# A GELU feed-forward block with its gradients on one core: four-tile transposing loads past the rows' ends, and another order of the opening loads

## The chip, the cores and the metric

The kernel runs on one core of one Trainium2 chip. The metric is the device time of one execution in microseconds; the median of three runs before the change is 280.55 us (280.51 to 280.58).

## The reference

```python
def _fwd_reference(x, w1, b1, w2, b2):
    h = jnp.einsum("bsd,df->bsf", x, w1) + b1
    h = _gelu(h)                       # tanh form
    return jnp.einsum("bsf,fd->bsd", h, w2) + b2

def reference(x, w1, b1, w2, b2, grad_out):
    _out, _vjp = jax.vjp(_f, x, w1, b1, w2, b2)
    _grads = _vjp(grad_out)
    return (_out, *_grads)
```

All arrays are bf16: x and grad_out (g below) 1 x 2048 x 448, w1 448 x 1792, w2 1792 x 448, b1 1792, b2 448. Six outputs are wanted: the forward result, and the gradients of x, w1, b1, w2 and b2.

## The kernel before

**Sizes.** The 2048 rows are cut into four blocks of 512 (SB). F = 1792 is 14 tiles of 128, taken as 7 pairs. D = 448 is three full tiles and a tail of 64 (KF = 3, DL = 64). One step is one pair of one block, so there are 28 steps.

**A step.** With u = x w1 + b1 and q = g w2^T (both held transposed, F on the partitions), step i issues on PE: the full tiles of u for step i + 2 (L159), the tails of that u and of q of step i (L169, L174; contractions over 64 rows, which sit in different halves of the array), the full tiles of q (L184), and then some matmuls of finished pairs for output rows (`ps_o`) and x-gradient rows (`ps_x`), both L255. ACT copies u out of PSUM with the bias (L193) and makes gelu(u) into `hT` (L199), a square (L203) and a tanh (L211). DVE makes the derivative of gelu from these (L207 to L220), and L224 multiplies it with q out of PSUM into `ghT`. Two PSUM buffers of the pool `psq` are used in turn, in effect one for u and one for q: q of step i + 1 can start only when L224 of step i has read q of step i, and u of a step when the copies of the one before are done. The order is written out by hand (a manual schedule), and each engine works through its own instructions in that order.

**Loads.** x and g are needed with D on the partitions, w2 too. Each of these is brought by transposing DMAs on SP's queue: one for the three full tiles, and one for the tail, whose 128 columns overlap the full tiles by 64 (L90 and L91 for x, L97 and L98 for g, L109 and L110 for w2). In `xT` the tail of x lies in partitions 64 to 127; in `gT` and `w2T_t` the tail lies in partitions 0 to 63. w1 (L102, with its 64 tail rows by L103) and w2 as it is (`w2_sb`, L106) come by plain loads. All of them are issued in program order on SP's queue, apart from w1's first two parts, which ACT's queue issues. `w1T_sb` (w1 transposed, L138) is first needed by the x gradient. Eight semaphores are used in turn for the loads of SP and ACT: a load is issued only when the eighth before it has landed.

**Opening.** Ten matmuls on zeros (L143) warm PE up. Then u of steps 0, 1 and 2, output matmuls of pair 0, q of step 0, output matmuls of pair 1, and the loop over steps 1 to 27. In the first block every step takes the next pair of w1, of w2 transposed and of w2, so each part of the weights has a step at which it is first wanted.

**Later.** `turn_gh` (L236) turns finished pairs of `ghT` by transposing DMAs into `gh_nat`; gelu results are stored to DRAM by POOL's queue (L231) and read back transposed (L382). The next blocks of x and g are loaded in steps 8, 10, 14 and 16. After step 27 come the rest of the output and x-gradient rows, then the gradient of w1 (L430, L441) and that of w2 (L454).

Of the kernel before, what the change touches and what calls it, by code (L numbers as in the profile page):

```python
# [19 lines left out]
def kernel(  # L20
# [15 lines left out]
    nc = tc.nc  # L36
# [12 lines left out]
    NSTEP = NB * NPAIR  # L49
    LEAD = 2  # L50
    SYNC_DEP = mybir.DependencyInfo(mybir.DependencyClass.Sync, mybir.DependencyReason.DATA)

# [22 lines left out]
    w1_f = const.tile([P, KF, F], BF16, name="w1_f")  # L75
    w2T_f = const.tile([P, KF, F], BF16, name="w2T_f")
    wt1 = const.tile([P, F], BF16, name="wt1")
    w2T_t = const.tile([P, F], BF16, name="w2T_t")
    w2_sb = const.tile([P, NF, D], BF16, name="w2_sb")
# [5 lines left out]
    xT, gT = {}, {}  # L85

    def load_x(b):
        t = blk.tile([P, KF + 1, SB], BF16, name="xT", tag="xT")
        rows = slice(b * SB, (b + 1) * SB)
        nc.sync.dma_start_transpose(out=t[:, 0:KF, :], in_=x2[rows, 0:KF * P])  # L90
        nc.sync.dma_start_transpose(out=t[:, KF, :], in_=x2[rows, D - P:D])  # L91
        xT[b] = t

    def load_g(b):
        t = blk.tile([P, KF + 1, SB], BF16, name="gT", tag="gT")
        rows = slice(b * SB, (b + 1) * SB)
        nc.sync.dma_start_transpose(out=t[:, 0:KF, :], in_=g2[rows, DL:D])  # L97
        nc.sync.dma_start_transpose(out=t[:, KF, :], in_=g2[rows, 0:P])  # L98
        gT[b] = t

    def load_w1(eng, f0, f1):
        eng.dma_start(out=w1_f[:, :, f0:f1], in_=w1[0:KF * P, f0:f1].rearrange("(kt p) f -> p kt f", p=P))  # L102
        eng.dma_start(out=wt1[DL:P, f0:f1], in_=w1[KF * P:D, f0:f1])  # L103

# [3 lines left out]
    def load_w2T(f0, f1):  # L108
        nc.sync.dma_start_transpose(out=w2T_f[:, :, f0:f1], in_=w2[f0:f1, DL:D])  # L109
        nc.sync.dma_start_transpose(out=w2T_t[:, f0:f1], in_=w2[f0:f1, 0:P])  # L110

# [29 lines left out]
    pw = psu.tile([P, SB], F32, name="pw", tag="pu")  # L141
    for i in range(10):
        nc.tensor.matmul(pw[:], lhsT=zero[:, 0:P], rhs=zero[:], start=True, stop=True)  # L143
# [5 lines left out]
    U, A, Z, PU, PQ = {}, {}, {}, {}, {}  # L149

    def pe_u_fulls(f):
        b, p = divmod(f, NPAIR)
        if p == 0:
            hT[b] = blk.tile([P, NF, SB], BF16, name="hT", tag="hT")
        PU[f] = psq.tile([P, 2, SB], F32, name="pu", tag="pq")
        for a in range(2):
            fc = slice((2 * p + a) * P, (2 * p + a + 1) * P)
            for kt in range(KF):
                nc.tensor.matmul(PU[f][:, a, :], lhsT=w1_f[:, kt, fc], rhs=xT[b][:, kt, :], start=(kt == 0), stop=False,  # L159
                                 skip_group_check=True)  # L160

    def pe_tails(f, k):
        if k is not None:
            PQ[k] = psq.tile([P, 2, SB], F32, name="pq", tag="pq")
        for a in range(2):
            if f is not None:
                b, p = divmod(f, NPAIR)
                fc = slice((2 * p + a) * P, (2 * p + a + 1) * P)
                nc.tensor.matmul(PU[f][:, a, :], lhsT=wt1[DL:P, fc], rhs=xT[b][DL:P, KF, :], start=False, stop=True,  # L169
                                 tile_position=(DL, 0), skip_group_check=True)  # L170
            if k is not None:
                b, p = divmod(k, NPAIR)
                fc = slice((2 * p + a) * P, (2 * p + a + 1) * P)
                nc.tensor.matmul(PQ[k][:, a, :], lhsT=w2T_t[0:DL, fc], rhs=gT[b][0:DL, KF, :], start=True, stop=False,  # L174
                                 tile_position=(0, 0), skip_group_check=True)

    def pe_q_fulls(k):
        b, p = divmod(k, NPAIR)
        if p == 0:
            ghT[b] = blk.tile([P, NF, SB], BF16, name="ghT", tag="ghT")  # L180
        for a in range(2):
            fc = slice((2 * p + a) * P, (2 * p + a + 1) * P)
            for kt in range(KF):
                nc.tensor.matmul(PQ[k][:, a, :], lhsT=w2T_f[:, kt, fc], rhs=gT[b][:, kt, :], start=False, stop=(kt == KF - 1),  # L184
                                 skip_group_check=True)

    def copy_u(f, engines):
        p = f % NPAIR
        U[f] = tmp.tile([P, 2, SB], BF16, name="U", tag="U", bufs=LEAD + 1)
        for a in range(2):  # L190
            bias = b1T[:, 2 * p + a:2 * p + a + 1]
            if engines[a] == "a":
                nc.scalar.activation(out=U[f][:, a, :], in_=PU[f][:, a, :], func=ACT.Identity, bias=bias)  # L193
            else:
                nc.vector.tensor_scalar(out=U[f][:, a, :], in0=PU[f][:, a, :], scalar1=bias, scalar2=None, op0=ALU.add)  # L195

    def act_gelu(f):
        b, p = divmod(f, NPAIR)
        nc.scalar.activation(out=hT[b][:, 2 * p:2 * p + 2, :], in_=U[f][:], func=ACT.Gelu_apprx_tanh)  # L199

# [12 lines left out]
    def dve_gate(k):  # L213
        b, p = divmod(k, NPAIR)
        a_, z_ = A[k], Z[k]
        nc.vector.tensor_scalar(out=a_[:], in0=a_[:], scalar1=GELU_C, scalar2=None, op0=ALU.add)
        nc.vector.tensor_tensor(out=a_[:], in0=a_[:], in1=hT[b][:, 2 * p:2 * p + 2, :], op=ALU.mult)
        nc.vector.tensor_scalar(out=a_[:], in0=a_[:], scalar1=-0.5, scalar2=None, op0=ALU.add)
# [3 lines left out]
    def dve_gh(k):  # L222
        b, p = divmod(k, NPAIR)
        gates[k] = nc.vector.scalar_tensor_tensor(out=ghT[b][:, 2 * p:2 * p + 2, :], in0=Z[k][:], scalar=1.0, in1=PQ[k][:],  # L224
                                       op0=ALU.add, op1=ALU.mult)

    gates = {}

    def store_h(f, after=None):
        b, p = divmod(f, NPAIR)  # L230
        st = nc.gpsimd.dma_start(out=hT_dram_v[:, 2 * p:2 * p + 2, b * SB:(b + 1) * SB], in_=hT[b][:, 2 * p:2 * p + 2, :])  # L231
        if after is not None:
            tc.add_manual_dep(st.ins, gates[after].ins.name, SYNC_DEP, reason="behind the loads of the first block")

    def turn_gh(b, p0, p1):
        nc.sync.dma_start_transpose(out=gh_nat[:, b, 2 * p0:2 * p1, :, :].rearrange("p ft j f -> p (ft j) f"),  # L236
                                    in_=ghT[b][:, 2 * p0:2 * p1, :].rearrange("p ft s -> p (ft s)"))

    class Unit:
# [9 lines left out]
        def emit(self, p):  # L249
# [3 lines left out]
            for a in range(2):  # L253
                ft = 2 * p + a
                nc.tensor.matmul(self.ps[:, 0:D], lhsT=src[self.b][:, ft, self.j * P:(self.j + 1) * P], rhs=w[:, ft, :],  # L255
                                 start=(ft == 0), stop=(ft == NF - 1 and not self.b2_pe),
                                 skip_group_check=True)
# [4 lines left out]
        def evict(self):  # L262
            st = stg.tile([P, SB], BF16, name="st", tag="st")
            r = self.b * SB + self.j * P
            if self.by_act:
# [62 lines left out]
    for i in range(1, NSTEP):  # L328
# [73 lines left out]
    def emit_sum(n):  # L402
        for _ in range(n):
# [10 lines left out]
            else:  # L414
                v = acc[:].rearrange("p (ft f) -> p ft f", f=P)
                b, j = divmod(st_, SPB)
                in0 = gh_nat[:, 0, :, 0, :] if st_ == 1 else v
                nc.vector.tensor_tensor(out=v, in0=in0, in1=gh_nat[:, b, :, j, :], op=ALU.add)  # L418
# [7 lines left out]
    def gw1_full(ft0, n, kt):  # L426
        ps = psu.tile([P, SB], F32, name="ps_w", tag="pu")
        for st_ in range(NS):
            b, j = divmod(st_, SPB)
            nc.tensor.matmul(ps[:, 0:n * P], lhsT=x_nat[:, st_, kt * P:(kt + 1) * P], rhs=gh_nat[:, b, ft0:ft0 + n, j, :],  # L430
# [5 lines left out]
    def gw1_tail(ft0, n):  # L436
        ps = psu.tile([P, SB], F32, name="ps_w", tag="pu")
        for st_ in range(NS):
            b, j = divmod(st_, SPB)
            for h in range(2):  # L440
# [62 lines left out]
```

## Time and profile before

| | |
|---|---|
| median of three runs | 280.55 us |
| the profiled execution | 281.57 us, of which the span is 279.8 us |
| mean granted clock of PE | 0.994 |
| PE matmuls | 46.1 us `ps_o`, 44.8 `ps_x`, 42.2 u, 42.6 `ps_v`, 41.1 q, 36.7 `ps_w`; tails besides |
| DMA queues, share of 16 engines | SP 53.2%, POOL 12.1%, ACT 4.5% |
| packets of SP's queue | 96864, 28.86 MB |

The span runs from the first to the last instruction; times in the text are microseconds from its start. "SPq" is the issuing of DMAs on SP's queue, and the time given there is that of the issue; when a transfer has landed is told by its semaphore. A group's line gives start, length, engine, line, operation, tiles and number of instructions, and in brackets the idle time before it with what ended it. In a list of waits the numbers are the total, the number of times and the longest.

### The profile page before, as it was taken

How to read it: one execution, taken by the hardware profiler on the slowest of the kernel's cores; microseconds unless marked ns; L12 is line 12 of the kernel's file. 1: busy time of each engine (PE TensorE's matmuls, PEld its weight loads, DVE VectorE, ACT ScalarE, POOL GpSimd, SP SyncE). 2: the span in 40 equal slices, each digit the busy share in tenths (PEclk: the TensorE clock that was granted, in tenths of full speed). 3: DMA queues.
4: the chain of work that ended last, by engine and by line, in shares of the span. 5: the costliest groups of instructions: out<-in, count | busy, mean ns of one | idle time of the engine just before them, and what ended most of it. 6: DMA issues, size and time to landing. Idle time of an engine off the chain costs nothing.

```text
span 279.8 us, 3713 instructions
## 1 busy us (share of the span) xinstructions
PE 270.1 (97%) x1406; PEld 125.4 (45%) x1406; DVE 185.2 (66%) x275; ACT 141.4 (51%) x190; POOL 56.1 (20%) x73
## 2 busy tenths in 40 slices
PE   7999499999999999999999999999999999999995
PEld 2334134344444444444444444554444475555554
DVE  2588958799999999777979878205999994000000
ACT  2699738889798677777766670012111111111211
POOL 1000000625133130222311131121150005910000
PEclk9999979999999999999999999999999999999999
DMA  8989999999796844512934154999911111799951
GB/s 167 189 183 198 197 238 179 280 231 205 245 192 174 173 76 127 129 54 74 204 92 109 54 132 115 278 381 215 190 40 37 38 49 33 177 203 194 248 129 33
DMA packets 105922, 43.79 MB, mean 157 GB/s; under 512 B 90928, under 2 KB 103088, under 8 KB 105904
## 3 DMA queue, kind: packets, MB, share of 16 engines
q1 hardware_dynamic: 96864, 28.86, 53.2%
q0 software_dynamic: 3872, 11.02, 12.1%
q10 hardware_dynamic: 5168, 3.67, 4.5%
q8 instruction: 11, 0.18, 0.3%
q14 instruction: 7, 0.06, 0.1%
HBM read 7.00 MB, written 14.23 MB: 76 GB/s over the span
## 4 chain that ended last, share of the span: by engine, by line
PE 86%; SPq 8%; DMA 4%; ACT 1%; issue 0%
PE ps_x L255 15%; PE ps_v L454 15%; PE ps_o L255 13%; PE ps_w L430 13%; PE pq L184 12%; PE pu L159 11%; PE pu L169 4%; SPq L109 3%; PE ps_w L441 2%; DMA w_sb<-in_w_dram 2%; DMA xT<-in_x_dram 2%; SPq L110 2%; PE pq L174 1%; SPq L106 1%; SPq L103 1%; SPq L97 1%
## 5 line engine op out<-in xcount | busy, mean ns | idle before, releaser
L193 ACT ACTIVATE U<-pu,b1T 128x512 bf16<-128x512 f32 x55 | 34.8, 684 | 38.2 <-PE pu L169 38.2
L255 PE MATMUL ps_o<-w_sb,hT 128*128 128x448 bf16 x224 | 46.1, 354 | 3.6 <-DMA w_sb<-in_w_dram 3.6
L255 PE MATMUL ps_x<-w1T_sb,ghT 128*128 128x448 bf16 x224 | 44.8, 352 | 0.4 <-ACT st L266 0.4
L159 PE MATMUL pu<-xT,w_f 128*128 128x512 bf16 x168 | 42.2, 388 | 0.8 <-DMA xT<-in_x_dram 0.8
L454 PE MATMUL ps_v<-g_nat,h_nat 128*128 128x448 bf16 (+1 forms) x240 | 42.6, 340 | 0.0
L184 PE MATMUL pq<-gT,w2T_f 128*128 128x512 bf16 x168 | 41.1, 381 | 0.0
L224 DVE SCALAR_TENSOR_TENSOR ghT<-Z,pq 128x1024 bf16<-128x1024 bf16 x28 | 34.2, 1220 | 7.2 <-PE pq L184 5.3
L269 POOL DMA_DIRECT2D out_dram<-st x32 | 17.9, 562 | 98.5 <-ACT st L266 62.7
L430 PE MATMUL ps_w<-gh_nat,x_nat 128*128 128x512 bf16 (+1 forms) x192 | 36.7, 352 | 0.0
L255 PEld LDWEIGHTS <-hT 128*128 128x128 bf16 x224 | 21.7, 98 | 25.5 <-issue 3.8
L454 PEld LDWEIGHTS <-h_nat 128*128 128x128 bf16 x240 | 23.3, 98 | 19.3 <-issue 0.3
L255 PEld LDWEIGHTS <-ghT 128*128 128x128 bf16 x224 | 21.9, 98 | 21.7 <-issue 0.7
L231 POOL DMA_DIRECT2D hT_dram<-hT x28 | 20.2, 722 | 54.5 <-ACT Z L211 46.5
L418 DVE TENSOR_TENSOR acc<-acc,gh_nat 128x1792 f32<-128x1792 f32 x14 | 30.0, 2142 | 0.5
L199 ACT ACTIVATE hT<-U 128x1024 bf16<-128x1024 bf16 x28 | 29.8, 1064 | 0.4
L203 ACT ACTIVATE A<-U 128x1024 bf16<-128x1024 bf16 x28 | 29.4, 1051 | 0.8 <-DVE U L195 0.8
L211 ACT ACTIVATE Z<-Z 128x1024 bf16<-128x1024 bf16 x28 | 29.5, 1052 | 0.3 <-DVE Z L208 0.3
L430 PEld LDWEIGHTS <-x_nat 128*128 128x128 bf16 x192 | 18.7, 98 | 17.9 <-issue 0.4
L159 PEld LDWEIGHTS <-w_f 128*128 128x128 bf16 x168 | 16.6, 100 | 20.7 <-issue 3.6
L184 PEld LDWEIGHTS <-w2T_f 128*128 128x128 bf16 x168 | 14.1, 97 | 25.1 <-issue 11.9
L457 ACT CAST st<-ps_v 128x448 bf16<-128x448 f32 (+1 forms) x15 | 7.6, 507 | 34.8 <-PE ps_v L454 34.8
L433 ACT CAST st<-ps_w 128x512 bf16<-128x512 f32 (+1 forms) x12 | 6.4, 532 | 29.9 <-PE ps_w L430 29.9
(42 smaller groups left out, 215.9 us busy)
## 6 DMA issues: line engine op xcount, KB each, us to landing
hT_dram<-hT POOLq DMA_DIRECT2D x28, 256.0 KB, 4.4
out_dram<-st POOLq DMA_DIRECT2D x32, 112.0 KB, 4.3
x_nat<-in_x_dram SPq DMA_DIRECT2D x1, 1792.0 KB, 10.0
g_nat<-in_grad_out_dram SPq DMA_DIRECT2D x1, 1792.0 KB, 14.3
out_dram<-st ACTq DMA_DIRECT2D x13, 112.0 KB, 3.6
out_dram<-st ACTq DMA_DIRECT2D x9, 128.0 KB, 1.7
w_sb<-in_w_dram SPq DMA_DIRECT2D x4, 224.0 KB, 3.2
w_sb<-in_w_dram SPq DMA_DIRECT2D x1, 672.0 KB, 6.1
```

Of the source, the lines that this page charges most:

```text
L159: nc.tensor.matmul(PU[f][:, a, :], lhsT=w1_f[:, kt, fc], rhs=xT[b][:, kt, :], start=(kt == 0), stop=False, skip_group_check=True)
L184: nc.tensor.matmul(PQ[k][:, a, :], lhsT=w2T_f[:, kt, fc], rhs=gT[b][:, kt, :], start=False, stop=(kt == KF - 1), skip_group_check=True)
L193: nc.scalar.activation(out=U[f][:, a, :], in_=PU[f][:, a, :], func=ACT.Identity, bias=bias)
L199: nc.scalar.activation(out=hT[b][:, 2 * p:2 * p + 2, :], in_=U[f][:], func=ACT.Gelu_apprx_tanh)
L203: nc.scalar.activation(out=A[k][:], in_=U[k][:], func=ACT.Square, scale=math.sqrt(3.0 * GELU_A * GELU_C))
L211: nc.scalar.activation(out=Z[k][:], in_=Z[k][:], func=ACT.Tanh, scale=-1.0 / 3.0)
L224: gates[k] = nc.vector.scalar_tensor_tensor(out=ghT[b][:, 2 * p:2 * p + 2, :], in0=Z[k][:], scalar=1.0, in1=PQ[k][:], op0=ALU.add, op1=ALU ...
L231: st = nc.gpsimd.dma_start(out=hT_dram_v[:, 2 * p:2 * p + 2, b * SB:(b + 1) * SB], in_=hT[b][:, 2 * p:2 * p + 2, :])
L255: nc.tensor.matmul(self.ps[:, 0:D], lhsT=src[self.b][:, ft, self.j * P:(self.j + 1) * P], rhs=w[:, ft, :], start=(ft == 0), stop=(ft == NF ...
L418: nc.vector.tensor_tensor(out=v, in0=in0, in1=gh_nat[:, b, :, j, :], op=ALU.add)
L430: nc.tensor.matmul(ps[:, 0:n * P], lhsT=x_nat[:, st_, kt * P:(kt + 1) * P], rhs=gh_nat[:, b, ft0:ft0 + n, j, :], start=(st_ == 0), stop=(s ...
L454: nc.tensor.matmul(ps[:, 0:w], lhsT=h_nat[ft][:, st_, :], rhs=g_nat[:, st_, h * w:(h + 1) * w], start=(st_ == 0), stop=(st_ == NS - 1))
```

## The change

1. **Wide loads.** For blocks 0 and 1, x comes by one transposing load of four tiles of 128 columns: 512 elements per row from a row of 448, so that the last 64 are the start of the next row. g is read from 64 elements ahead of each row, so that its tail lies in the upper half of tile 0, and w2 transposed likewise. `w2T` is one tile of four parts. Blocks 2 and 3 keep two loads each.
2. **Halves swapped.** With this the tail of x lies in partitions 0 to 63 and that of g and w2 in 64 to 127 for blocks 0 and 1. For blocks 2 and 3 the operands are wanted in the other halves: `other_halves`, issued by POOL at step 9, brings w1's tail rows a second time and copies w2T's tail from one half to the other.
3. **Rotations.** The blocks go over the rows in the order 512, 1024, 1536, 0 and the pairs in the order 1 to 6, 0, so that no wide load runs past the ends of x, g or w2. w2T's first 16 rows of w2 can't be read from 64 elements ahead; they come by a narrow transposing load and a plain load of 64 x 16 single elements.
4. **Order of the opening loads.** ACT issues w1's columns 256 to 511, and, behind the warm activation with its table load, 512 to 767 (the second and third part). On SP each part of w2 goes ahead of later parts of w2T, tiles 8 to 11 of w2 ahead of w1's last part; w2T's first part is last, behind x of block 1.
5. **Others.** Nine warm-up matmuls instead of ten. `turn_gh` splits its last call of each block, since pair 0 is not next to pair 6.

```diff
+    ROW0 = [SB, 2 * SB, 3 * SB, 0]
+    WIDE = (0, 1)
+    FP = [1, 2, 3, 4, 5, 6, 0]
...
+    def wide(src, r0, n, shift):
+        return bass.AP(src.tensor, src.offset + r0 * D - shift, [[D, n], [1, (KF + 1) * P]])
+
     def load_x(b):
         t = blk.tile([P, KF + 1, SB], BF16, name="xT", tag="xT")
-        rows = slice(b * SB, (b + 1) * SB)
-        nc.sync.dma_start_transpose(out=t[:, 0:KF, :], in_=x2[rows, 0:KF * P])
-        nc.sync.dma_start_transpose(out=t[:, KF, :], in_=x2[rows, D - P:D])
+        r0 = ROW0[b]
+        if b in WIDE:
+            nc.sync.dma_start_transpose(out=t[:], in_=wide(x2, r0, SB, 0))
+        else:
+            nc.sync.dma_start_transpose(out=t[:, 0:KF, :], in_=x2[r0:r0 + SB, 0:KF * P])
+            nc.sync.dma_start_transpose(out=t[:, KF, :], in_=x2[r0:r0 + SB, D - P:D])
...
     def load_w2T(f0, f1):
-        nc.sync.dma_start_transpose(out=w2T_f[:, :, f0:f1], in_=w2[f0:f1, DL:D])
-        nc.sync.dma_start_transpose(out=w2T_t[:, f0:f1], in_=w2[f0:f1, 0:P])
+        if f0 > 0:
+            nc.sync.dma_start_transpose(out=w2T[:, :, f0:f1], in_=wide(w2, f0, f1 - f0, DL))
+        else:
+            nc.sync.dma_start_transpose(out=w2T[:, :, 16:f1], in_=wide(w2, 16, f1 - 16, DL))
+            nc.sync.dma_start_transpose(out=w2T[:, 1:KF + 1, 0:16], in_=w2[0:16, DL:D])
+            nc.sync.dma_start(out=w2T[DL:P, 0, 0:16], in_=w2[0:16, 0:DL].rearrange("f d -> d f"))
...
     load_x(0)
-    load_w1(nc.scalar, 0, 256)
     load_w1(nc.scalar, 256, 512)
     warm = stg.tile([P, 1], F32, name="warm", tag="warm", bufs=1)
     nc.scalar.activation(out=warm[:], in_=zero[:, 0:1], func=ACT.Gelu_apprx_tanh)
-    load_w1(nc.sync, 512, 768)
-    load_w2(nc.sync, 0, 2)
+    load_w1(nc.scalar, 512, 768)
+    load_w1(nc.sync, 768, 1024)
+    load_w2(nc.sync, 2, 4)
     load_g(0)
-    load_w2T(0, 256)
-    load_w2(nc.sync, 2, 4)
-    load_w1(nc.sync, 768, 1024)
     load_w2T(256, 512)
     load_w2(nc.sync, 4, 6)
     load_w1(nc.sync, 1024, 1280)
-    load_w2T(512, 1024)
+    load_w2T(512, 768)
     load_w2(nc.sync, 6, 8)
-    load_w1(nc.sync, 1280, F)
-    load_w2T(1024, F)
-    load_w2(nc.sync, 8, NF)
+    load_w1(nc.sync, 1280, 1536)
+    load_w2T(768, 1280)
+    load_w2(nc.sync, 8, 12)
+    load_w1(nc.sync, 1536, F)
+    load_w1(nc.sync, 0, 256)
+    load_w2(nc.sync, 12, NF)
+    load_w2(nc.sync, 0, 2)
+    load_w2T(1280, F)
     nc.sync.dma_start(out=b2_bc[:], in_=b2.rearrange("(o d) -> o d", o=1).to_broadcast((P, D)))
     load_x(1)
+    load_w2T(0, 256)
     nc.sync.dma_start_transpose(out=w1T_sb[:], in_=w1[:, :])
     load_g(1)
...
-    for i in range(10):
+    for i in range(9):
...
+    def half(up):
+        return slice(DL, P) if up else slice(0, DL)
...
-                nc.tensor.matmul(PU[f][:, a, :], lhsT=wt1[DL:P, fc], rhs=xT[b][DL:P, KF, :], start=False, stop=True,
-                                 tile_position=(DL, 0), skip_group_check=True)
+                hf = half(b not in WIDE)
+                nc.tensor.matmul(PU[f][:, a, :], lhsT=wt1[hf, cols(p, a)], rhs=xT[b][hf, KF, :], start=False, stop=True,
+                                 tile_position=(hf.start, 0), skip_group_check=True)
...
+    def other_halves():
+        nc.gpsimd.dma_start(out=wt1[DL:P, :], in_=w1[KF * P:D, :])
+        nc.gpsimd.dma_start(out=w2T[0:DL, 0, :], in_=w2T[DL:P, 0, :])
...
     def turn_gh(b, p0, p1):
-        nc.sync.dma_start_transpose(out=gh_nat[:, b, 2 * p0:2 * p1, :, :].rearrange("p ft j f -> p (ft j) f"),
-                                    in_=ghT[b][:, 2 * p0:2 * p1, :].rearrange("p ft s -> p (ft s)"))
+        for q0, q1 in ([(p0, NPAIR - 1), (NPAIR - 1, NPAIR)] if p1 == NPAIR else [(p0, p1)]):
+            if q0 < q1:
+                ts = slice(2 * FP[q0], 2 * FP[q1 - 1] + 2)
+                nc.sync.dma_start_transpose(out=gh_nat[:, b, ts, :, :].rearrange("p ft j f -> p (ft j) f"),
+                                            in_=ghT[b][:, ts, :].rearrange("p ft s -> p (ft s)"))
...
+        if i == 9:
+            other_halves()
```

More of the change, by code (lines that the diff above doesn't have):

```diff
@@ L50 @@
     LEAD = 2
+    ROW0 = [SB, 2 * SB, 3 * SB, 0]
+    WIDE = (0, 1)
+    FP = [1, 2, 3, 4, 5, 6, 0]
+    PLACE = [((st // SPB - 1) % NB, st % SPB) for st in range(NS)]
     SYNC_DEP = mybir.DependencyInfo(mybir.DependencyClass.Sync, mybir.DependencyReason.DATA)
@@ L75 @@
     w1_f = const.tile([P, KF, F], BF16, name="w1_f")
-    w2T_f = const.tile([P, KF, F], BF16, name="w2T_f")
+    w2T = const.tile([P, KF + 1, F], BF16, name="w2T")
     wt1 = const.tile([P, F], BF16, name="wt1")
-    w2T_t = const.tile([P, F], BF16, name="w2T_t")
     w2_sb = const.tile([P, NF, D], BF16, name="w2_sb")
@@ L95, in load_g @@
         t = blk.tile([P, KF + 1, SB], BF16, name="gT", tag="gT")
-        rows = slice(b * SB, (b + 1) * SB)
-        nc.sync.dma_start_transpose(out=t[:, 0:KF, :], in_=g2[rows, DL:D])
-        nc.sync.dma_start_transpose(out=t[:, KF, :], in_=g2[rows, 0:P])
+        r0 = ROW0[b]
+        if b in WIDE:
+            nc.sync.dma_start_transpose(out=t[:], in_=wide(g2, r0, SB, DL))
+        else:
+            nc.sync.dma_start_transpose(out=t[:, 1:KF + 1, :], in_=g2[r0:r0 + SB, DL:D])
+            nc.sync.dma_start_transpose(out=t[:, 0, :], in_=g2[r0:r0 + SB, 0:P])
         gT[b] = t
@@ L102, in load_w1 @@
         eng.dma_start(out=w1_f[:, :, f0:f1], in_=w1[0:KF * P, f0:f1].rearrange("(kt p) f -> p kt f", p=P))
[L103 removed]
+        eng.dma_start(out=wt1[0:DL, f0:f1], in_=w1[KF * P:D, f0:f1])
     def load_w2(eng, t0, t1):
@@ L181, in pe_q_fulls @@
         for a in range(2):
-            fc = slice((2 * p + a) * P, (2 * p + a + 1) * P)
-            for kt in range(KF):
-                nc.tensor.matmul(PQ[k][:, a, :], lhsT=w2T_f[:, kt, fc], rhs=gT[b][:, kt, :], start=False, stop=(kt == KF - 1),
+            for kt in range(1, KF + 1):
+                nc.tensor.matmul(PQ[k][:, a, :], lhsT=w2T[:, kt, cols(p, a)], rhs=gT[b][:, kt, :], start=False, stop=(kt == KF),
                                  skip_group_check=True)
@@ L198, in act_gelu @@
         b, p = divmod(f, NPAIR)
-        nc.scalar.activation(out=hT[b][:, 2 * p:2 * p + 2, :], in_=U[f][:], func=ACT.Gelu_apprx_tanh)
+        nc.scalar.activation(out=hT[b][:, pair(p), :], in_=U[f][:], func=ACT.Gelu_apprx_tanh)
     def act_square(k):
@@ L253, in emit @@
             for a in range(2):
-                ft = 2 * p + a
+                ft = 2 * FP[p] + a
                 nc.tensor.matmul(self.ps[:, 0:D], lhsT=src[self.b][:, ft, self.j * P:(self.j + 1) * P], rhs=w[:, ft, :],
-                                 start=(ft == 0), stop=(ft == NF - 1 and not self.b2_pe),
+                                 start=(p == 0 and a == 0),
+                                 stop=(p == NPAIR - 1 and a == 1 and not self.b2_pe),
                                  skip_group_check=True)
```

33 lines of the change are left out of this document (18 added, 15 removed).

## The prediction

> **What bounds the kernel now.** I read the page first. PE is busy for 97% of the span at nearly full clock, and the chain that ended last is 86% PE; so only PE's idle time and its slow stretches can be won.
>
> ```profile
> span 279.8 us, 3713 instructions
> PE 270.1 (97%) x1406; PEld 125.4 (45%) x1406; DVE 185.2 (66%) x275; ACT 141.4 (51%) x190; POOL 56.1 (20%) x73
> PEclk9999979999999999999999999999999999999999
> ```
>
> Then the list of PE's waits, which is short:
>
> ```profile
> PE ps_o L255 <- DMA w_sb<-in_w_dram: 3.6, 1, 3.6
> PE pw L143 <- DVE zero L112: 1.2, 1, 1.2
> PE pu L159 <- DMA xT<-in_x_dram: 0.8, 1, 0.8
> PE pq L174 <- ACT U L193: 0.6, 1, 0.6
> ```
>
> One wait matters: the w2 load of tiles 8 to 13, the last of the weights on SP's queue. The timeline of PE shows the wait and what follows it:
>
> ```profile
> 29.24 1.47 PE L184 MATMUL pq<-gT,w2T_f 128*128 128x512 bf16 x6
> 34.27 1.97 PE L255 MATMUL ps_o<-w_sb,hT 128*128 128x448 bf16 x8 [3.56 <-DMA w_sb<-in_w_dram]
> 36.03 2.77 PE L159 MATMUL pu<-xT,w_f 128*128 128x512 bf16 x6
> 42.16 1.03 PE L159 MATMUL pu<-xT,w_f 128*128 128x512 bf16 x4
> ```
>
> After it the same six L159 take 2.77 us instead of 1.47: the windows give a granted clock of 0.76, 0.50, 0.50 and 0.54 from 35 to 39. By the starts of groups, L255 lost 0.25, L159 1.31 and the tails 0.07: 1.6 us. The stall and its clock cost 5.2 us.
>
> SP's timeline says why the load is late. Short transposes cost 1.25 us of issue even for one tile, and large ones block:
>
> ```profile
> 0.73 1.36 SPq L90 DMA_TRANSPOSE xT<-in_x_dram  x1
> 2.15 1.39 SPq L91 DMA_TRANSPOSE xT<-in_x_dram  x1
> 10.20 1.24 SPq L110 DMA_TRANSPOSE w2T_t<-in_w_dram  x1
> 22.11 4.68 SPq L109 DMA_TRANSPOSE w2T_f<-in_w_dram  x1
> 26.84 1.27 SPq L110 DMA_TRANSPOSE w2T_t<-in_w_dram  x1
> 28.16 0.58 SPq L106 DMA_DIRECT2D w_sb<-in_w_dram  x1
> ```
>
> SP issues without pause from 0.73 to 47 us. From 10 to 20 the queues moved 159 GB/s; beside the big w1 transpose, from 39 to 42, they moved 290. So issue, not the transfers, holds back the first half.
>
> Last, DVE, which would be late next:
>
> ```profile
> 28.61 0.43 DVE L207 TENSOR_SCALAR Z<-A 128x1024 bf16<-128x1024 bf16 x1
> 32.45 1.22 DVE L224 SCALAR_TENSOR_TENSOR ghT<-Z,pq 128x1024 bf16<-128x1024 bf16 x1
> 33.78 0.43 DVE L207 TENSOR_SCALAR Z<-A 128x1024 bf16<-128x1024 bf16 x1
> 40.85 1.22 DVE L224 SCALAR_TENSOR_TENSOR ghT<-Z,pq 128x1024 bf16<-128x1024 bf16 x1 [3.34 <-PE pq L184]
> ```
>
> Its step lasts 33.78 - 28.61 = 5.17 us without a gap, PE's in block 0 only 27.31 - 22.56 = 4.75. DVE is hidden now because PE stands still.
>
> **The w2 wait.** Six transposes fewer go out up to w2's tiles 8 to 13 (x, g and four w2T tails), some 7.5 us of issue; and tiles 8 to 11 are now asked for ahead of w1's last part, w1's first part, and the last two w2T. Adding issues (1.3 for a 256-column transpose, 0.46 to 0.58 for a plain load, 2 to 2.5 for 2048 rows of tile, from L236's shortest, 1.8 to 3.1), they go out at about 16.4 and land 3.4 later, near 20. PE wants them at 25.8 on the old clock of steps. A check by bytes: 4.4 MB lie up to and with that load; at the 190 GB/s of the old opening they are through at 2.7 + 23.1 = 25.8, at 290 at 18. So the wait is at most some tenths even at the old rate. The later needs (w1 tiles 10 to 13, w1 first part, last w2T at 33.8) have 3 us or more by issue. The stall goes.
>
> By the Trainium skill (DMA: Bandwidth & Descriptors, "Issuing engines are not separate DMA queues"), the time a sequencer takes to start a DMA is usually small beside the DMA, so merging issues should bring little. The rows differ here: 1.24 us of issue for 64 KB that need 0.2 us at 290 GB/s. By that rule the old rate stays, and the time would come out as in the third rival.
>
> **What is late next.** PE's q of step 4 needs the PSUM buffer that DVE's L224 of step 3 frees at 32.45 + 1.22 = 33.67. PE is ready at 30.55 + 1.51 (o) + 1.39 (u) = 33.45. From there PE follows DVE: L224 starts at 32.45, 37.62, 42.79 and 47.96 for steps 3 to 6, against 32.45, 40.85, 46.63 and 51.87 before. That is 3.9 us at step 6, not 5.2. In step 7 DVE idled 1.53 us before L207 at 54.62, waiting for ACT behind four evictions. In the new order that chain ends so: step 5's L224 ends at 44.0, tails 0.6, copies 1.3, evictions 1.7, gelu 1.0, square 1.05, so L207 at 49.8, where DVE is free at 49.3: 0.5 idle instead of 1.5. L224 of step 7 then starts at 49.8 + 3.84 = 53.6 against 58.46: 4.8. With small semaphore gaps counted, **4.65 us**. From step 7 on both are paced alike (DVE 5.17, PE 5.13), and the 6.26 us steps and the weight gradients move as a block.
>
> **The start.** PE's first matmul waits for x. Before, the three-tile load landed 5.3 us after its issue, at 6.05; the fourth tile's load, not needed until 7.58, no longer counts. One load of four tiles moves 0.13 MB more ahead of the first matmul: 0.45 us at 290 GB/s, 0.8 at 159. The two weight loads on ACT that raced with it now come later, behind the table load (1.28). Bounds: -0.6 (the race was all of the tail) to +1.5 (twice the slower rate). I take **+0.5**, PE at 6.6. Everything hangs on this, since ACT's and DVE's chain begins at u of step 0. w1's third part, by ACT at 3.3, lands after 4.3 to 4.9 at 7.6 to 8.8; PE wants it at 8.5 and its tail at 9.9: nothing, or 0.3.
>
> The warm-up loses one matmul, 0.41 us, which is time before x lands: nothing, if the clock holds. Idle before u would be 6.6 - 4.9 = 1.7 us. 0.81 us did no harm, 3.56 did. The Trainium skill (TensorE: Matmul & The Clock Gate, "Part 1") lets the clock fall after an idle window of some 3.4 us; the 3.56 us here agree, and by it 1.7 keeps the clock.
>
> **Tails.** In blocks 0 and 1 the halves are swapped for both operands; in steps 12 and 13 u is of block 2 (upper half) while q is of block 1 (upper half too). Four tails in different halves take 0.54 us a step; two tails alone in the same half took 0.53 (7.58 to 8.11). So 2 x 0.53 = 1.06 at most, 0 if PE waits for DVE anyway; I take **0.3**, since PE is on DVE's pace in these steps.
>
> **Moved elsewhere.** POOL gets two loads at step 9 (0.7 us of issue each); behind them are h stores, wanted at the end, and x-gradient stores with six staging buffers. They land in 6 to 8 us, near 70; the first tail that reads them comes at 76: nothing. The gradient turns get 4 more issues on SP, each 1.3; the last turn becomes shorter (8 tiles after step 27, not 16), and x_nat lands 6 us ahead of need (185.5 against 191.5): nothing. x of block 1 (before at 37.2), w1T (44.0) and g of block 1 (46.8) must come by 37.7, 46.9 and 50.8. SP gets through there at about 27, 37 and 39, landings 31, 39.5 and 42.5: nothing. w2T's first part now stands ahead of w1T with 64x16 single elements, 1024 packets, 64 to an engine. At the page's mean packet, 0.532 x 279.8 x 16 / 96864 = 24.6 ns, that is 1.6 us, inside 7.4 us of slack.
>
> **Sum.** -4.65 + 0.5 + 0.3 = -3.85. The profiled execution took 281.57 (span 279.8); the median is 280.55, 1.02 less. 281.57 - 3.85 = 277.7 profiled, **276.7** as a median.
>
> **Rivals.**
> - More: x lands no later or sooner and the tails hide: 4.65 + 0.6 = 5.25, **275.3**. For: the wide load ends a race of three queues. Against: more bytes ahead of the first matmul. 0.12.
> - Clock: the 1.7 us gap lets PE fall to half clock for one stretch of 3.4 us, as from 35.5 to 38.9. Its 1.6 us are then on ACT's and DVE's chain: **278.3**. 0.08.
> - The wide load does not do what it says (issue takes as long as the two that it replaces, ring full): the old rate, the last w2T lands at 34.4 where it is wanted, others a little late, 0.5 to 2.5 us: **277.2 to 279.2**. 0.09.
> - Slower: the single-element load blocks SP's queue ahead of w1T. It decides when it takes more than 1.6 + 7.4 + 3.85, some 13 us: 0.2 us a packet, eight times the mean. At 0.3 us (19.2), w1T lands at 57.1, PE stands still for 10.2: **287**. For: no row shows a packet of 2 bytes. Against: everything else small is far cheaper. 0.10, taking in any like block on the queue.
> - No change within 0.2% (0.56 us, about what a measurement of this kernel can tell from none): gain and a new wait cancel, 280.5. 0.03.
>
> **How the numbers follow.** The forecast case has 0.58. Faster: 0.58 + 0.12 + 0.08 + 0.09 = 0.87; same 0.03; slower 0.10. The range goes from the first rival, 275.1, to the late end of the third, 279.3.
>
> **What would show it.** PE's waits without the w2 load; granted clock 1.0 from 30 to 40; DVE without a gap from step 2 to 6 and PE waiting about 0.4 us for L224 before q in steps 4 and 5; the first matmul near 6.6; SP past w2's tiles 8 to 11 by 17; tails of 1.0 us in steps 12 and 13. A first matmul after 8, a wait for w1T or for w2T's first part, or a half clock at the start would make it wrong.

## The result, and the profile after

The changed kernel took 277.24 us in the median (277.38, 277.05, 279.10, 277.10) and the kernel before, beside it, 280.53 (280.58, 280.55, 280.51, 280.35): a ratio of 0.9899 [0.9856, 0.9941], 3.3 us less. The profiled execution took 277.38 with a span of 275.6, against 281.57 and 279.8: 4.19 less, where the prediction's sum was 3.85.

The page after. It has no clock row, since this trace holds no clock record at all; that the clock was full is read from the lengths of the matmuls below:

```profile
span 275.6 us, 3712 instructions
PE 268.6 (97%) x1391; PEld 125.7 (46%) x1405; DVE 185.5 (67%) x275; ACT 141.4 (51%) x190; POOL 57.7 (21%) x75
```

The waits of PE (total, times, longest, in us). The w2 load, 3.6 before, is no longer among them, and nothing has come in its place:

```profile
PE pw L162 <- DVE zero L128: 1.2, 1, 1.2
PE pu L183 <- DMA xT<-in_x_dram: 1.1, 1, 1.1
PE pq L201 <- ACT U L219: 0.6, 1, 0.6
PE ps_x L288 <- ACT st L300: 0.3, 1, 0.3
```

The timeline of PE where the stall was (start, busy time, instructions). The output matmuls follow q at once, and u takes 1.46 again, not 2.77. The two tails that shared their time are now 0.28 apart, because q's tail waits for a PSUM buffer:

```profile
29.26 1.47 PE L210 MATMUL pq<-gT,w2T 128*128 128x512 bf16 x6
30.56 1.68 PE L288 MATMUL ps_o<-w_sb,hT 128*128 128x448 bf16 x8
32.08 1.46 PE L183 MATMUL pu<-xT,w_f 128*128 128x512 bf16 x6
33.47 0.39 PE L196 MATMUL pu<-xT,wt 64*128 64x512 bf16 x1
33.75 0.37 PE L201 MATMUL pq<-gT,w2T 64*128 64x512 bf16 x1
```

The timeline of DVE shows who holds that buffer. L250 is the old L224; its starts are those of steps 3 to 7:

```profile
32.48 1.22 DVE L250 SCALAR_TENSOR_TENSOR ghT<-Z,pq 128x1024 bf16<-128x1024 bf16 x1
...
37.64 1.22 DVE L250 SCALAR_TENSOR_TENSOR ghT<-Z,pq 128x1024 bf16<-128x1024 bf16 x1
39.39 0.43 DVE L233 TENSOR_SCALAR Z<-A 128x1024 bf16<-128x1024 bf16 x1 [0.53 <-DVE ghT L250]
43.23 1.22 DVE L250 SCALAR_TENSOR_TENSOR ghT<-Z,pq 128x1024 bf16<-128x1024 bf16 x1
...
48.46 1.22 DVE L250 SCALAR_TENSOR_TENSOR ghT<-Z,pq 128x1024 bf16<-128x1024 bf16 x1
49.96 0.43 DVE L233 TENSOR_SCALAR Z<-A 128x1024 bf16<-128x1024 bf16 x1 [0.28 <-ACT A L229]
54.01 1.22 DVE L250 SCALAR_TENSOR_TENSOR ghT<-Z,pq 128x1024 bf16<-128x1024 bf16 x1
```

Step 7 comes at 54.01 and not 58.46: 4.45 us won there. The weight gradients begin at 187.35 instead of 191.36, so 4.0 us are left there, and 4.2 at the end.

The timeline of SP (its issues): one load for x and one for g, and the load of w2's tiles 8 to 11 is issued at 17.06, where before's last w2 load stood at 28.16:

```profile
0.73 1.42 SPq L97 DMA_TRANSPOSE xT<-in_x_dram  x1
...
4.54 3.23 SPq L107 DMA_TRANSPOSE gT<-in_grad_out_dram  x1
...
14.05 2.97 SPq L122 DMA_TRANSPOSE w2T<-in_w_dram  x1
17.06 0.59 SPq L118 DMA_DIRECT2D w_sb<-in_w_dram  x1
```

And the start of PE, where the nine warm-up matmuls and the first real ones stand:

```profile
1.18 3.92 PE L162 MATMUL pw<-zero 128*128 128x512 bf16 x9 [1.18 <-DVE zero L128]
6.21 1.46 PE L183 MATMUL pu<-xT,w_f 128*128 128x512 bf16 x6 [1.10 <-DMA xT<-in_x_dram]
```

### The profile page after: what moved, and what is told of

The parts are those of the page before. It is cut to its first block, busy times and chain, and to the rows that moved or that the text cites. A ratio compares the mean times of both kernels' runs of the same rounds, so it can differ in the third digit from the quotient of the medians.

```text
span 275.6 us, 3712 instructions
## 1 busy us (share of the span) xinstructions
PE 268.6 (97%) x1391; PEld 125.7 (46%) x1405; DVE 185.5 (67%) x275; ACT 141.4 (51%) x190; POOL 57.7 (21%) x75
## 4 chain that ended last, share of the span: by engine, by line
PE 85%; DVE 6%; ACT 6%; DMA 2%; issue 1%; DVEq 0%
PE ps_x L288 15%; PE ps_v L490 15%; PE ps_w L466 13%; PE ps_o L288 12%; PE pq L210 11%; PE pu L183 10%; PE pu L196 4%; PE ps_w L477 2%; ACT U L219 2%; DMA xT<-in_x_dram 2%; ACT A L229 1%; DVE ghT L250 1%; PE pq L201 1%; ACT hT L225 1%; DVE Z L234 1%; DVE Z L246 1%
## 5 line engine op out<-in xcount | busy, mean ns | idle before, releaser
L183 PE MATMUL pu<-xT,w_f 128*128 128x512 bf16 x155 | 40.0, 379 | 1.7 <-DMA xT<-in_x_dram 1.1
L210 PE MATMUL pq<-gT,w2T 128*128 128x512 bf16 x167 | 40.9, 381 | 0.2 <-issue 0.2
L303 POOL DMA_DIRECT2D out_dram<-st x32 | 18.3, 573 | 95.3 <-ACT st L300 59.9
L250 DVE SCALAR_TENSOR_TENSOR ghT<-Z,pq 128x1024 bf16<-128x1024 bf16 x28 | 34.2, 1220 | 4.4 <-PE pq L210 2.0
L210 PEld LDWEIGHTS <-w2T 128*128 128x128 bf16 x168 | 14.1, 98 | 25.1 <-issue 11.8
```

Source lines behind the costliest of these rows:

```text
L183: nc.tensor.matmul(PU[f][:, a, :], lhsT=w1_f[:, kt, cols(p, a)], rhs=xT[b][:, kt, :], start=(kt == 0), stop=False, skip_group_check=True)
L210: nc.tensor.matmul(PQ[k][:, a, :], lhsT=w2T[:, kt, cols(p, a)], rhs=gT[b][:, kt, :], start=False, stop=(kt == KF), skip_group_check=True)
L250: gates[k] = nc.vector.scalar_tensor_tensor(out=ghT[b][:, pair(p), :], in0=Z[k][:], scalar=1.0, in1=PQ[k][:], op0=ALU.add, op1=ALU.mult)
```

## The experiments

The theory was the prediction's: the w2 load stood last on SP, its wait cost PE time and clock, and DVE's pace takes a part of the gain back. The rivals left to tell apart: that the order of the loads does it, or their width; and, for the runs near 279 that the changed kernel shows (279.10 in the four above), that they come from the copies of step 9 or from the clock at the start. The runs come in three sets, the first and third on one chip, the second on another. The kernel before had medians of 278.85, 280.42 and 280.53 in them, so times and ratios are compared within a set, and across sets only with a word of caution.

**The changed kernel again**, without an edit (first set, as the next three).

> The changed kernel again, beside the others. Its four runs so far were 277.05, 277.10, 277.38 and 279.10. If the two wide copies of step 9 now and then land after step 12 wants them (72.7 against 75.9 in the profile), some runs lie about 2 us higher and most near 277.1; if 279.10 was a single accident, all lie within 0.4 us.

277.32 in the median of 12 runs, ratio 0.9924 [0.9889, 0.9960]. Ten runs lie from 276.94 to 277.67; two took 278.75 and 279.06. The profile has no w2 wait, but x landed at 5.82 and the first six matmuls of u took 2.06 us, not 1.46. So the gain holds, and the start is not the same in every run.

**The order alone**, on the kernel before, with its narrow loads and ten warm-up matmuls:

```diff
-    load_w2(nc.sync, 6, 8)
-    load_w1(nc.sync, 1280, F)
-    load_w2T(1024, F)
-    load_w2(nc.sync, 8, NF)
+    load_w2(nc.sync, 6, 10)
+    load_w1(nc.sync, 1280, 1536)
+    load_w1(nc.sync, 1536, F)
+    load_w2(nc.sync, 10, NF)
+    load_w2T(1024, 1536)
...
     load_x(1)
+    load_w2T(1536, F)
```

> The kernel before with the new order of the opening loads alone: w2's tiles 6 to 9 and 10 to 13 ahead of w2T's later parts, w1's last part in two, w2T's last part behind x of block 1; all loads narrow, no rotation, halves as before. Theory (order and merged issues each do nearly the whole): the wait for w2 goes, PE falls in with DVE's pace; the narrow loads then bring w1T at about 47 and g of block 1 at about 50, just when they are wanted (46.8 and 50.1): 276.9 to 278.3. Rival (the gain needs the merged issues): w2, w1T or g come 2 us or more late and it stays above 279.

277.02 (276.68 to 277.30, 12 runs), ratio 0.9911 [0.9881, 0.9942]. No w2 wait is left. The loads land later than in the changed kernel (x of block 1 at 34.4 instead of 31.3, w1T at 43.5 instead of 41.3), and nobody waits for them. By the time, the order alone brings all that the change brings; and since its tails keep their halves, it has no price to pay in steps 12 and 13.

**The width alone**: the changed kernel with w2's tiles 10 to 13 last again.

```diff
-    load_w2(nc.sync, 8, 12)
+    load_w2(nc.sync, 8, 10)
     load_w1(nc.sync, 1536, F)
     load_w1(nc.sync, 0, 256)
-    load_w2(nc.sync, 12, NF)
-    load_w2(nc.sync, 0, 2)
     load_w2T(1280, F)
+    load_w2T(0, 256)
+    load_w2(nc.sync, 10, NF)
+    load_w2(nc.sync, 0, 2)
```

> The changed kernel with the wide loads, the rotations and the swapped halves, but its opening loads in the order of before (w2's tiles 10 to 13 and 0 to 1 last, behind w2T, the narrow part of w2T ahead of them). Theory: by the issue times of the changed kernel's trace w2's tiles 10 and 11 land at 31 to 32, wanted at 30.6, where 0.3 to 0.4 us is spent on DVE anyway: 277.0 to 278.2. Rival (the gain needs the order): a wait of 2.5 us or more for w2, 279.5 or above.

277.31 (277.00 to 278.98, 12 runs, two of them near 279), ratio 0.9939 [0.9909, 0.9970]. The timeline of PE shows the wait again, but short, and with no loss of clock after it:

```profile
31.46 1.67 PE L288 MATMUL ps_o<-w_sb,hT 128*128 128x448 bf16 x8 [0.71 <-DMA w_sb<-in_w_dram]
```

It costs nothing that the time shows (277.31 against 277.32): L250 of step 7 starts at 54.07, against 54.01 in the changed kernel, so PE would have waited for DVE a moment later anyway. The last run below has a longer wait, which is not free. By the time, either half of the change is enough.

**No halves to share and no copies**: every block of x and g is loaded wide, with short loads for the 16 rows that can't be, so that the tails of x always lie in the lower and those of g in the upper half.

```diff
-        if b in WIDE:
+        if b != 2:
             nc.sync.dma_start_transpose(out=t[:], in_=wide(x2, r0, SB, 0))
...
-                hf = half(b not in WIDE)
+                hf = half(False)
...
-                hf = half(b in WIDE)
+                hf = half(True)
...
-        if i == 9:
-            other_halves()
```

> The changed kernel with wide loads in all four blocks: the 16 rows at the end of x (block 2) and at the start of g (block 3) come by a narrow transpose and a plain load of single elements, as w2T's first rows do; the halves are the same in all blocks, so the two copies of step 9 are gone and the tails of steps 12 and 13 no longer share a half. Theory: the tails take 0.54 again instead of 0.96, worth 0.1 to 0.8 us as DVE leaves it; the queues move at their usual rate from 66 to 74; 276.4 to 277.1, and no run near 279 if the copies made that one. Rival (the copies cost nothing, DVE hides the tails): 277.0 to 277.3, and the spread of runs stays.

276.68 (276.52 to 276.76, 6 runs), ratio 0.9886 [0.9835, 0.9938]: 0.64 below the changed kernel of the same set, and no run of the two overlaps. The price of the shared half is seen in the changed kernel's timeline of PE, step 12, where the four tails stand one after the other:

```profile
74.55 1.46 PE L183 MATMUL pu<-xT,w_f 128*128 128x512 bf16 x6
75.94 0.39 PE L196 MATMUL pu<-xT,wt 64*128 64x512 bf16 x1
76.16 0.38 PE L201 MATMUL pq<-gT,w2T 64*128 64x512 bf16 x1
76.38 0.38 PE L196 MATMUL pu<-xT,wt 64*128 64x512 bf16 x1
76.59 0.38 PE L201 MATMUL pq<-gT,w2T 64*128 64x512 bf16 x1
76.90 1.47 PE L210 MATMUL pq<-gT,w2T 128*128 128x512 bf16 x6
```

From the first tail to q that is 0.96 us instead of 0.54; step 13 has the same (81.49 to 82.46). In this kernel the tails run in pairs (75.61 and 75.66, 75.83 and 75.88). The edit takes away the shared half and the copies together. In the profiles, the multiplies that make `ghT` run 0.3 us ahead of the changed kernel's up to step 15 and 0.72 ahead from step 16 on. So 0.4 of the 0.64 can be put down to the tails; the first 0.3 stand there from the start, where x happened to land at 5.66 and not at 6.16, and what makes the rest in the other runs was not separated.

**DVE's share** (second set, as the next three): the kernel above without one addition. It leaves out the constant that L216 adds in block 0, so its derivative of gelu is not the reference's there, and DVE's step is shorter.

```diff
-        nc.vector.tensor_scalar(out=a_[:], in0=a_[:], scalar1=GELU_C, scalar2=None, op0=ALU.add)
+        if k >= NPAIR:
+            nc.vector.tensor_scalar(out=a_[:], in0=a_[:], scalar1=GELU_C, scalar2=None, op0=ALU.add)
```

> The kernel with wide loads in all blocks (276.68), leaving out in block 0 the addition of a constant to A on DVE (0.43 us, one of eight DVE operations of a step), so that the derivative of gelu is not that of the reference there. Theory (DVE's 5.17 us a step sets PE's pace from step 2 to 7): a step of DVE is 4.72, under PE's 4.75, PE no longer waits for L250 before q of steps 4 and 5, and 0.7 to 1.0 us is gained: 275.7 to 276.0. Rival (PE's own work or ACT sets the pace): within 0.2 us of 276.68.

276.00 (6 runs), ratio 0.9871 [0.9828, 0.9914]. Five runs lie from 275.70 to 276.12, some 0.7 below the kernel above, which stands in another set. The traces say the same without that doubt. L254, the counterpart of L250, comes every 4.71 us in steps 2 to 4, and not every 5.17:

```profile
28.39 1.22 DVE L254 SCALAR_TENSOR_TENSOR ghT<-Z,pq 128x1024 bf16<-128x1024 bf16 x1
...
33.10 1.22 DVE L254 SCALAR_TENSOR_TENSOR ghT<-Z,pq 128x1024 bf16<-128x1024 bf16 x1
```

From step 0 to step 7 this multiply takes 36.70 us, against 37.61 in the kernel above, and PE no longer waits for it before its tails. So DVE held PE in block 0. The sixth run, 277.64, is the profiled one, and the timeline of its PE shows the other matter:

```profile
1.18 4.02 PE L165 MATMUL pw<-zero 128*128 128x512 bf16 x9 [1.18 <-DVE zero L131]
6.16 2.72 PE L186 MATMUL pu<-xT,w_f 128*128 128x512 bf16 x6 [0.96 <-DMA xT<-in_x_dram]
```

x lands as in the changed kernel, but its first matmuls run at half clock. The trace's clock records grant full clock only at 9.51 us.

**The copies later**: behind step 10, not step 9.

```diff
-        if i == 9:
+        if i == 10:
             other_halves()
```

> The changed kernel with the two wide copies for the other halves one step later, behind step 10. Theory (their landing at 72.7 to 75.5 is close to 75.9 to 76.2, where the tail of u in step 12 wants w1's tail rows, and the runs near 279 are those in which it is later): the copies land 2 to 5 us after they are wanted, PE waits before that tail in every run, 278.5 to 281.5, and the wait stands in the list of PE's waits. Rival (the copies have nothing to do with the slow runs): 277.0 to 277.5, with one run in seven near 279.

278.24 (276.99 to 282.65, 12 runs), ratio 0.9946 [0.9909, 0.9982]. The wait of some microseconds that was expected in every run did not come: the issue moved only from 63.9 to 65.3, the copies landed at 76.50 and 77.20, and PE waited 0.3 for them in the profiled run. Two runs took 280.78 and 282.65, with a mean clock of 0.994 where the other ten have 0.999 or 1.000; by their clock they lost a stretch of full clock somewhere, perhaps after a longer wait for the copies, but they were not profiled. The five runs from 278.02 to 278.84 may hold more than the copies: in the profiled one (278.02) full clock was granted only at 7.02 us. So this run does not tell the two causes apart.

**The copies earlier**: behind step 7.

```diff
-        if i == 9:
+        if i == 7:
             other_halves()
```

> The changed kernel with the two wide copies two steps earlier, behind step 7. Theory: they land near 65 to 68, 8 us ahead of need; no run near 279, all within 0.4 us, and what is left against the version with wide loads in all blocks (276.68) is the price of the tails of steps 12 and 13 that share a half: 276.8 to 277.2. Rival (the slow runs have another cause): one run in seven still near 279.

277.35 (277.04 to 279.02, 8 runs), ratio 0.9927 [0.9890, 0.9964]. The copies landed at 59.9 and 61.8, far ahead of need, and two of the runs still took 278.89 and 279.02. The runs near 279 don't come from late copies.

**The addition on GpSimd** for steps 2 to 6, in the kernel without shared halves:

```diff
+        if 2 <= k < NPAIR:
+            BP[k] = gh_nat[:, 3, 2 * (k % 2):2 * (k % 2) + 2, :, :].rearrange("p a j f -> p a (j f)")
+            nc.gpsimd.tensor_scalar(out=BP[k], in0=A[k][:], scalar1=GELU_C, scalar2=None, op0=ALU.add)
```

> The kernel with wide loads in all blocks, where for steps 2 to 6 the addition of a constant to A is done by GpSimd, idle there, into a part of gh_nat that is not yet used, in place of DVE. Nothing is left out. Theory: as in the run that leaves the addition out, 0.5 to 1.0 us gained, 275.7 to 276.2, if GpSimd takes less than 4 us for 128x1024 and does not slow DVE. Rival: GpSimd's operation slows DVE's beside it or comes too late for L243, no gain or a loss, 276.7 to 280.

276.42 (11 runs), ratio 0.9884 [0.9852, 0.9916]: eight runs from 276.17 to 276.75, three at 278.14 to 278.17. DVE's step is 4.71 again in steps 2 to 4. The timeline of POOL gives the price there, 2.77 for what takes DVE 0.43, and the first two of these additions took 3.00:

```profile
29.56 2.77 POOL L239 TENSOR_SCALAR gh_nat<-A 128x1024 bf16<-128x1024 bf16 x1 [1.48 <-ACT A L232]
```

By the eight runs it gains about 0.3 on the version with all loads wide, less than the 0.7 of leaving the addition out. The sets differ, but the traces agree: from step 0 to step 7 the multiply into `ghT` takes 37.21 us, so 0.40 of the 0.91 above is kept. Where the rest goes stands in DVE's timeline:

```profile
22.30 1.40 DVE L242 TENSOR_TENSOR Z<-Z,U 128x1024 bf16<-128x1024 bf16 x1
```

It runs beside the first GpSimd addition (21.91 to 24.91) and takes 1.40 instead of 0.69; the same happens at 25.50, beside the second. So the rival, that GpSimd slows DVE, held for two of the five additions. Beside the other three nothing took twice its time; the reason is open.

**Seven warm-up matmuls** in the changed kernel (third set, as the rest):

```diff
-    for i in range(9):
+    for i in range(7):
```

> The changed kernel with seven warm-up matmuls on zeros in place of nine. Theory (the runs near 279 are those in which PE's clock is not yet granted when x lands: in two slow profiles the grant came at 9.5, behind a stretch of 3.41 us in which PE was busy for 2.5 us, in others it came after stretches with 2.75 us or more): the gap before u grows to 1.6 to 2 us, and most runs are slow, the median 278.3 to 279.5, the fastest still near 277. Rival (the copies make the slow runs): as with nine, one run in six near 279, median 277.3.

278.66 in the median of 12 runs, ratio 0.9919 [0.9891, 0.9947]: eight runs from 278.51 to 279.24, and four from 276.87 to 277.26. Two warm-up matmuls fewer make the late clock, rare with nine, the usual case, and the copies are the same in both.

**Eleven** of them:

```diff
-    for i in range(9):
+    for i in range(11):
```

> The changed kernel with eleven warm-up matmuls. Theory (clock at the start): they end at 5.3 to 5.9, the gap before u is under 0.5 us, no stretch of 3.41 us has less than 2.9 us of work, and no run lies near 279: 276.8 to 277.5. Rival (the copies): one run in six near 279.

277.31, ratio 0.9882 [0.9849, 0.9915]; five of six runs from 277.19 to 277.59, none near 279. One took 286.08 with a mean clock of 0.988. It was not profiled; that its copies landed late is possible, and open.

**All that helped**: the kernel with the addition on GpSimd and eleven warm-up matmuls.

> Wide loads in all blocks, the addition of steps 2 to 6 on GpSimd, and eleven warm-up matmuls. By the parts: 276.2 to 276.6 in all runs, none near 278 (with nine matmuls three of eleven were); if the slow runs had another cause, some stay at 278.2.

276.60 (276.40 to 277.02, 6 runs), ratio 0.9858 [0.9828, 0.9888]: below every run of the changed kernel with eleven matmuls in the same set, and of the kernel before. From the version that is only wide throughout (276.68, in another set) it can't be told apart.

**The kernel before, once more**, to see how steady its stall is:

> The kernel before again, for its profile on this chip, where its runs lie between 277.4 and 282.2. Theory: the wait for w2's last load and the half clock behind it differ from run to run (the load is last in a queue that is full), and the start's clock adds 0 or 2 us; the profile shows a w2 wait of 0 to 5 us that accounts for its time against 276.9 to 277.3 without one.

279.88 (278.01 to 280.64, 8 runs), ratio 0.9972 [0.9939, 1.0005] to the other runs of itself. The profile caught the run of 278.01. Its wait for w2 in the list of PE's waits, and what follows in the timeline:

```profile
PE ps_o L255 <- DMA w_sb<-in_w_dram: 1.3, 1, 1.3
```

```profile
32.34 1.67 PE L255 MATMUL ps_o<-w_sb,hT 128*128 128x448 bf16 x8 [1.31 <-DMA w_sb<-in_w_dram]
33.85 1.46 PE L159 MATMUL pu<-xT,w_f 128*128 128x512 bf16 x6
```

The same load landed at 32.30 and not 34.23, the stall is 1.3 instead of 3.6, and the six L159 after it take 1.46: no clock was lost. DVE's L224 then starts at 32.79, 37.96, 43.55, 48.78 and 54.91 in steps 3 to 7. Up to step 6 that is 0.31 or 0.32 behind the changed kernel in every step, and it was 0.31 already at step 0, where u ran partly at half clock (2.05 us for the first six). So up to step 6 the wait of 1.3 us on PE costs nothing, since DVE would have held PE anyway. At step 7 it is 0.90:

```profile
51.06 0.43 DVE L207 TENSOR_SCALAR Z<-A 128x1024 bf16<-128x1024 bf16 x1 [1.06 <-ACT A L203]
```

Here DVE idles 1.06 us for ACT's square, against 0.28 in the changed kernel. PE was still behind, u came to ACT later (46.14 instead of 45.04), and the square with it. So 0.59 of the 1.3 is paid after all, in a step where ACT and not DVE comes last.

## Why the prediction was right, and where it was off

**The w2 wait: right.** The load goes out at 17.06 (16.4 was said) and lands at 21.2 (near 20); the wait and the half clock after it are gone. Which part of the change does it was left open; the experiments say that the order does it alone, and the width nearly so. The rule of the Trainium skill that was weighed against this (DMA: Bandwidth & Descriptors, "Issuing engines are not separate DMA queues"), that starting a DMA usually takes the sequencer little time beside the DMA itself, was read to mean that merging issues brings little. That outcome is seen here: narrow loads in the new order took 277.02, wide ones 277.32. It is the landing that gains from the width: with w2 last in both, its wait was 0.7 with wide loads and 1.3 to 3.6 with narrow ones. The third rival, built on that rule, can't be told from the forecast by the time alone, since its 277.2 to 279.2 take in the measured 277.24. The trace tells them apart: x's wide load took 1.42 us of issue where the two took 2.75 (though g's took 3.23 where the two took 2.71), and nothing hangs on the issue rate once w2 stands ahead.

**What is late next: right.** L224 was to start at 32.45, 37.62, 42.79, 47.96 and 53.6; it did at 32.48, 37.64, 43.23, 48.46 and 54.01. The term of 4.65 measured 4.45 at step 7, or 4.57 without the 0.12 of the later start. The rest is one idle time of DVE that was not foreseen, 0.53 ahead of L233 at 39.39. It is in the narrow kernel too (37.40 to 42.99 is 5.59, not 5.17) and in before's run with the short stall (37.96 to 43.55). What DVE waits for there is open. Leaving out one of its operations showed that DVE's pace is the bound.

**The start: the term was mis-sized.** It was +0.5 with PE at 6.6; the wide load was issued in 1.42 us, landed at 6.16, and PE began at 6.21: +0.12. In the other profiles of wide loads x landed between 5.66 and 6.18. The prediction charged the fourth tile's bytes to the load at the queues' rate; the measured landing is that of the three-tile load of before, 6.05, within 0.11. The statement that w1's third part goes out at 3.3, behind the table load, was wrong also: it went out at 1.88, while the table load ran from 1.81 to 3.09. Nothing hung on it.

**Tails: right.** +0.3 was said; steps 12 and 13 spend 0.42 and 0.43 us more between the first tail and q, and the gain falls from 4.45 at step 7 to 4.0 at the weight gradients: about half of the 0.85 is hidden by DVE, as was said.

**Copies: right in most runs, with less margin than said.** They were to land near 70 and landed at 72.7 and 74.3, in another run the first at 75.46, with the first tail that reads them at 75.9 to 76.2. The windows from 66 to 74, of the changed kernel and then of the one without copies (the last column is GB/s), show that the queues move little while they run:

```profile
66.00:70.00 4.00, 3.95 (x21) 1.89 (x21) 3.76 (x8) 3.77 (x5) 1.66 (x3) 1.00 1.30 124
70.00:74.00 4.00, 4.00 (x22) 1.68 (x21) 3.76 (x8) 3.08 (x6) 0.65 (x1) 1.00 1.09 62
```

```profile
66.00:70.00 4.00, 3.95 (x20) 1.96 (x20) 3.79 (x7) 3.97 (x5) 0.16 (x1) 1.00 1.14 222
70.00:74.00 4.00, 4.00 (x22) 1.65 (x21) 3.76 (x8) 3.08 (x6) 0.95 (x2) 1.00 1.17 189
```

**The single-element load: the fear was unfounded.** Its 1024 packets of 2 bytes took 8.5 ns each, not 24.6, and it landed 3.7 us after its issue. The slower rival needed 0.2 us a packet.

**From the profiled run to the median: the step that was off.** The sum was carried to the median by taking off 1.02, the difference between before's profiled run and its median, as if it were a constant of the measurement. In the changed kernel it is not there: its profiled run (277.38) and its median (277.24) agree. Without the 1.02 the forecast was 277.7, with it 276.7, and the median lies halfway between. That the 1.02 were stall is likely and not shown, since only two of before's runs were profiled. The one of 281.57 had a stall of 3.6 and one stretch of 3.41 us at half clock behind it, the one of 278.01 a stall of 1.3 and no such stretch. The mean clock of before's runs sorts them: over the three sets, 30 runs have 1.000 and medians of 278.5 to 279.0, 39 have 0.994 and 280.6, six have 0.988 and 282.1 to 282.3. A step of 0.006 is 1.7 us, which is what one such stretch costs.

So what the change brings is 3.4 us against a run of before that lost a stretch (280.6), and 1.3 against one that lost none (278.5). In the first set, where most of before's runs lost none, it brings 1.5 us (278.85 to 277.32). That a gain of 3.85 was forecast and 3.3 measured owes something to luck: the three runs of before that the forecast started from and the four that stood beside the result all took 280.35 to 280.58, as its runs with a lost stretch do.

**The warm-up: right in most runs only.** "Nothing, if the clock holds" asked whether an idle time of 1.7 us lets the clock fall. That was the wrong question: at the gap full clock may not have been granted yet. The clock records of the traces are always whole multiples of 3.413 us apart (30.72, 242.35, 266.24 and 269.65 us are 9, 71, 78 and 79 of them), with another phase in each run. Full clock was first granted at 4.79 us in before, 4.33 with eleven matmuls, 7.12 in the changed kernel's second profile and 9.51 in the one without the addition. Reckoned back by one stretch of 3.413 us, it was granted after stretches in which PE was busy for 2.75 us or more (3.70 to 7.12 in that second profile: 1.49 of warm-up and 1.26 of u). It was not granted after 2.52 (2.68 to 6.10 in the one without the addition) or 2.55 (0.31 to 3.73 in before's run of 278.01). The gap between the warm-up and x's landing, 0.5 to 1.1 us with nine matmuls, decides it where a boundary falls badly. Then u of step 0 runs at half clock, and the run ends 1.6 to 2.0 us later.

So the clock rival (278.3) is no alternative to the forecast: something near it is what about one run in five of the kernels with nine matmuls does (by their times 1 of 4, 2 of 12, 2 of 12, 0 of 6, 1 of 6, 2 of 8 and 3 of 11, the kernel with the later copies left aside). It is what eight of 12 do with seven, none of 12 with ten and the new order, and none of 12 in the two kernels with eleven. The section of the Trainium skill that was cited for the idle time (TensorE: Matmul & The Clock Gate, "Part 1") also states the half that was left out: the array starts throttled, and the window of some 3.4 us runs freely, so the change-over differs from run to run. These runs agree, with 3.413 us.

The reading of before's clock was too simple as well. The prediction said that the idle 3.56 us agree with an idle window of some 3.4. Reckoned in the same stretches, none was idle throughout: the clock fell at 35.51, after stretches with 2.02 and 1.24 us of work. In the run of 278.01 a single stretch with 2.10 us of work did not let it fall.

**Small slips.** The range was built from 275.1 and 279.3, where the rivals themselves say 275.3 and 279.2; nothing hangs on it.

## What to carry to other kernels

A stall that one profiled run shows is one draw: before it is priced, look at the mean clock and the time of every run, since the same wait measured 1.3 and 3.6 us here, and the larger one also cost the clock. Price its removal by what holds the engine next: here DVE's pace hid a wait of 0.7 us on PE, and more than half of one of 1.3. And let warm-up matmuls run up to the moment the data lands, since one stretch with too little work in it cost 1.6 to 2.0 us here, and two matmuls more showed no price.

## What the runs showed of the hardware that was not expected

- The first grant of full clock depends on the phase of 3.413 us stretches and on how full one is: 2.75 us of work was enough, 2.55 was not. The windows print a clock of 1.00 ahead of the first record, and throughout where a trace has no record, so a late grant is read from the matmuls' lengths (2.72 us for six instead of 1.46).
- The two plain copies landed 9.1 and 10.1 us after their issue. Their 64 packets of 7168 bytes took from 0.27 to 4.32 us each, half of them under 0.51, where most packets of 4096 took 0.16 to 0.19. The queues fell to 62 GB/s from 70 to 74 us, a turn of the gradient landed 19.5 us after its issue, and still PE waited for none of it in the changed kernel. Issued behind step 7, the same packets took 0.40 us in the mean. What slows them was not tried.
- 1024 packets of 2 bytes cost 8.5 ns each on the queues.
- A DMA of ACT was issued at 1.88 us while its table load ran (1.81 to 3.09).
- An addition of 128 x 1024 took GpSimd 2.77 to 3.00 us, and DVE 0.43. Beside two of the five, an operation of DVE took 1.40 us instead of 0.69.
